# Linear attention and two MLPs on one core: the first MLP's weights converted two chunks at a time, all their lo parts on VectorE, and k's maximum as a tree

## The chip, the cores and the metric

The kernel runs on one core of one Trainium2 chip. The metric is the device time of one execution in microseconds (us); lower is better. The engines are named as in the profile: PE is TensorE's matmul, PEld its weight load, DVE VectorE, ACT ScalarE, POOL GpSimd, SP SyncE, which here only issues transfers (SPq).

## The reference, cut to what matters

```python
q_s = softmax(q, axis=-1); k_s = softmax(k, axis=2)      # (4, 8, 576, 64); over head_dim, over positions
kv = einsum("bhsd,bhse->bhde", k_s, v)
x = einsum("bhsd,bhde->bhse", q_s, kv)  -> (2304, 512)
x = (h - tanh(h)) @ moe_w_out,    h = x @ moe_w_in       # first MLP, d_ff 2048
x = softplus(h) @ moe2_w_out,     h = x @ moe2_w_in      # second MLP, same sizes
```

The weights reach the kernel as float64. All is computed to float32 accuracy: each matmul operand is split into a hi part in the rounded format float32r and a lo part, the float32 remainder, and each product is three matmuls (lo*hi, hi*lo, hi*hi).

## The kernel before, in words

The 2304 tokens are cut into five blocks of 512, 256, 512, 512 and 512. The first MLP walks through the blocks, and in each through d_ff in 16 chunks of 128 (a step is one chunk of one block). A step has 12 matmuls for the hidden layer (`hidden`, L323), the gate h - tanh(h) with its hi and lo part (`gate`, L332 to L335: ACT, DVE, ACT, DVE), and 12 matmuls that add the chunk to the block's output in four PSUM accumulators (`mid_out`, L350 to L352). `hidden` runs two steps ahead of `mid_out`. After the first MLP comes the second, which uses a Strassen-like scheme for its first matmul and takes the rest of the time.

The first block is also where the first MLP's weights are made. `w_task(f)` loads chunk f of `w_in` and of `w_out` as 64-bit words into two buffers of the tag "raw" (six of them, 4 KB per partition each), and two steps later turns each into float32 with `convert`: ACT writes sign and exponent material into the low words y (L121), DVE merges it with the sign of the high words x (L122), clamps x (L123), ACT scales x (L124), DVE shifts and merges (L125). `parts` then splits the float32 words: ACT copies the hi part (L131), and lo = x - hi (L132) runs on POOL, except for `w_in` of every fourth chunk, which runs on DVE. All of these work on 128 x 512 elements. The raw buffer is free once lo is done, and the next load into it waits for that on SP's queue. All weights stay in SBUF: `weights_out` holds `w_out`, the pools "first", "mid" and "last" hold `w_in`. The last two, and the pool "x1", lie where the prologue's tiles were.

In the fifth block, `w2_out_task` loads and converts the second MLP's `w_out` in the same way into the places of the first's, with lo on POOL (L155). In blocks three and four, `w2_in_task` converts the second `w_in`, builds its seven forms and writes them to DRAM (L189).

Attention for the next block runs beside the MLP's steps: `kv_task` (two heads each, four per batch) takes the maximum of k over positions in two stages. The first is a `tensor_reduce` on DVE over the six rows j that a partition holds (L229, 96 x 768 to 96 x 128, reading with j innermost, i.e. strided); then a transpose, a reduction over partitions, exp and the matmuls with v. `x_task` does q's softmax and multiplies by kv. A prologue does both for the first block, in an order written out by hand (`order`, L553), in which w0 and w1 are the conversions of chunks 0 and 1. Its x_tasks run two operations each on POOL (L281, L289).

Each engine works through its own queue in a fixed order, which the framework's planner sets at build time by the order of the program and the readiness of operands in its own cost model. Semaphores hold an instruction until its operands are there, and everything behind it on that engine waits too. `at(block, step, make)` says at which step a task starts; `yield` ends a task's share of a step.

Of the kernel before, what the change touches and what calls it, by code (L numbers as in the profile page):

```python
# [9 lines left out]
F32 = mybir.dt.float32  # L10
F32R = mybir.dt.float32r
U32 = mybir.dt.uint32
U16 = mybir.dt.uint16
AF = mybir.ActivationFunctionType
ALU = mybir.AluOpType
AX = mybir.AxisListType.X
# [3 lines left out]
def linear_attention_two_mlps(  # L20
# [28 lines left out]
    nc = tc.nc  # L49
    B, H, S, D = q.shape  # L50
    NT, DM = out.shape
    DFF = w1_in.shape[1] // 2
    P = 128
# [5 lines left out]
    NC = DM // P  # L59
    NF = DFF // P  # L60
    NHP = H // 2
    KP, KJ = 96, 6
# [26 lines left out]
    def f32(ap):  # L89
        return ap.bitcast(F32)  # L90
# [6 lines left out]
    weights = {}  # L97
    wi, wo = {}, {}

    def raw_tile(name):  # L100
        return main.tile([P, NC, 2 * P], U32, tag="raw", name=name, bufs=6)

    def load_in(raw, w_in, f):
        nc.sync.dma_start(
            out=raw, in_=w_in[:, 2 * f * P : 2 * (f + 1) * P].rearrange("(c p) f -> p c f", p=P)
        )

    def load_out(raw, w_out, f):
        nc.sync.dma_start(out=raw.rearrange("p c f -> p (c f)"), in_=w_out[f * P : (f + 1) * P, :])

    def convert(raw):

        words = raw.rearrange("p c (f two) -> p c f two", two=2)
        y, x = words[:, :, :, 0], words[:, :, :, 1]
        top = raw.bitcast(U16).rearrange("p c (f four) -> p c f four", four=4)[:, :, :, 1]  # L120
        nc.scalar.activation(y, top, AF.Copy, scale=2.0**-13, bias=2.0**-14 - 0.5)  # L121
        nc.vector.scalar_tensor_tensor(y, x, 0x80000000, y, op0=ALU.bitwise_and, op1=ALU.bitwise_or)  # L122
        nc.vector.tensor_scalar(f32(x), f32(x), MOST, -MOST, op0=ALU.min, op1=ALU.max)  # L123
        nc.scalar.mul(f32(x), f32(x), 2.0**-111)  # L124
        nc.vector.scalar_tensor_tensor(x, x, 3, y, op0=ALU.logical_shift_left, op1=ALU.bitwise_or)  # L125
        return f32(x)

    def parts(pool, w, m, f, x, eng):
        hi = pool.tile([P, NC, P], F32R, tag=f"{w}h{f}", name=f"{w}h{m}_{f}")
        lo = pool.tile([P, NC, P], F32R, tag=f"{w}l{f}", name=f"{w}l{m}_{f}")  # L130
        nc.scalar.copy(hi, x)  # L131
        eng.tensor_tensor(lo, x, f32(hi), op=ALU.subtract)  # L132
        return hi, lo

    def whole(t):
        return t.rearrange("p c f -> p (c f)")

    def w_task(f):
        raws = [raw_tile(f"raw{w}0_{f}") for w in "io"]
        load_in(raws[0], w1_in, f)  # L140
        load_out(raws[1], w1_out, f)
        yield
        yield
        pool = weights["first" if f < 4 else "last" if f >= 12 else "mid"]
        wi[f] = parts(pool, "i", 0, f, convert(raws[0]), nc.vector if f % 4 == 0 else nc.gpsimd)
        wo[0, f] = tuple(map(whole, parts(weights_out, "o", 0, f, convert(raws[1]), nc.gpsimd)))

    def w2_out_task(f):
        raw = raw_tile(f"rawo1_{f}")
        load_out(raw, w2_out, f)  # L150
        yield
        yield
        x = convert(raw)
        yield
        wo[1, f] = tuple(map(whole, parts(weights_out, "o", 1, f, x, nc.gpsimd)))  # L155

    forms = [dram.tile([P, NFORM, 2, 2 * P], F32, tag=f"forms{p}", name=f"forms{p}") for p in range(NF // 2)]

    def w2_in_task(p):


        raws = [raw_tile(f"rawi1_{f}") for f in PAIRS[p]]
        for raw, f in zip(raws, PAIRS[p]):
            load_in(raw, w2_in, f)
        yield
        yield
        w0 = convert(raws[0])
        yield
        w1 = convert(raws[1])
        yield  # L170
        sums = f32(raw_tile(f"sums{p}").rearrange("p c f -> p (c f)")).rearrange("p (s c f) -> p s c f", s=4, c=2)
        s2, s3, s1, s4 = (sums[:, i] for i in range(4))
        a11, a12, a21, a22 = w0[:, :2], w0[:, 2:], w1[:, :2], w1[:, 2:]
        nc.vector.tensor_tensor(s1, a21, a22, op=ALU.add)
        nc.vector.tensor_tensor(s2, s1, a11, op=ALU.subtract)
        nc.vector.tensor_tensor(s3, a11, a21, op=ALU.subtract)
        nc.vector.tensor_tensor(s4, a12, s2, op=ALU.subtract)
        yield
        flat = sums.rearrange("p s c f -> p s (c f)")
        for n, of in enumerate((w0, flat[:, :2], flat[:, 2:], a22)):  # L180
            size = 1 if n == 3 else 2
            t = main.tile([P, size, 2, 2 * P], F32R, tag="raw", name=f"stage{p}_{n}", bufs=6)
            hi, lo = t[:, :, 0], t[:, :, 1]
            if n in (0, 3):
                hi, lo = (v.rearrange("p s (c f) -> p s c f", c=2) for v in (hi, lo))
                of = of.rearrange("p (s c) f -> p s c f", c=2)
            nc.scalar.copy(hi, of)
            nc.vector.tensor_tensor(lo, of, f32(hi), op=ALU.subtract)
            nc.sync.dma_start(out=forms[p][:, 2 * n : 2 * n + size], in_=f32(t))  # L189
            yield  # L190
# [11 lines left out]
    def kv_task(b, hp, pool, bufs):  # L202


        nm = f"{b}_{hp}"

        def load(t, src):
            for h in range(2):
                nc.sync.dma_start(
                    out=t[:, :, h * D : (h + 1) * D], in_=src[b, 2 * hp + h].rearrange("(p j) d -> p j d", j=KJ)  # L210
                )

        if pool is att:
            kt = ke = pool.tile([KP, KJ, 2, D], F32, tag="k", name=f"k{nm}", bufs=bufs)
            load(kt.rearrange("p j h d -> p j (h d)"), k)
        else:
            whole = pool.tile([KP, 2, KJ, D], F32, tag="k", name=f"k{nm}", bufs=bufs)
            nc.sync.dma_start(
                out=whole.rearrange("p h j d -> p h (j d)"),
                in_=k[b, 2 * hp : 2 * hp + 2].rearrange("h (p j) d -> p h (j d)", j=KJ),  # L220
            )
            kt = whole.rearrange("p h j d -> p j h d")
            ke = pool.tile([KP, KJ, 2, D], F32, tag="ke", name=f"ke{nm}", bufs=bufs)
        yield
        vt = pool.tile([KP, KJ, P + 2], F32, tag="v", name=f"v{nm}", bufs=bufs)
        nc.gpsimd.memset(vt[:, :, P:], 1.0)
        load(vt, v)
        m1 = pool.tile([KP, 2, D], F32, tag="m1", name=f"m1{nm}", bufs=bufs)
        nc.vector.tensor_reduce(m1, kt.rearrange("p j h d -> p h d j"), axis=AX, op=ALU.max)  # L229
        yield  # L230
        pm = psum_a(f"pm{nm}")
        nc.tensor.transpose(pm[:, :KP], m1.rearrange("p h d -> p (h d)"), ident[:KP, :KP])
        mx = pool.tile([P, 1], F32, tag="mx", name=f"mx{nm}", bufs=bufs)
        nc.vector.tensor_reduce(mx, pm[:, :KP], axis=AX, op=ALU.max)
        yield
        pb = psum_a(f"pb{nm}")
        nc.tensor.transpose(pb[:KP, :P], mx.to_broadcast([P, KP]), ident)
        most = pb[:KP, :P].rearrange("p (h d) -> p h d", h=2).unsqueeze(1).to_broadcast([KP, KJ, 2, D])
        nc.vector.tensor_tensor(ke, kt, most, op=ALU.subtract)
        nc.scalar.activation(ke, ke, AF.Exp)  # L240
        yield
        pk = psum_a(f"pk{nm}")
        for j in range(KJ):
            nc.tensor.matmul(pk[:, : P + 2], ke[:, j].rearrange("p h d -> p (h d)"), vt[:, j], start=j == 0, stop=j == KJ - 1)
        r = pool.tile([P, 1], F32, tag="r", name=f"r{nm}", bufs=bufs)
        nc.vector.tensor_scalar(r, pk[:, P : P + 1], 1e-9, None, op0=ALU.add)
        nc.vector.reciprocal(r, r)
        for h in range(2):
            d = slice(h * D, (h + 1) * D)
            nc.scalar.mul(kv[b % 2, hp][d, d], pk[d, d], r[d])  # L250
# [268 lines left out]
    def at(block, step, make):  # L519
        starts.setdefault(block * NF + step, []).append(make)  # L520

    PRE = 2
    KV_AT, X_AT = (0, 3, 6, 9), (1, 4, 8, 10)
    for f in range(NF):
        if f >= PRE:
            at(0, f - 6, lambda f=f: w_task(f))
        if f < NF - 2:
            at(NB - 1, f - 1, lambda f=f: w2_out_task(ORDER[f]))
    for p in range(NF // 2):
# [19 lines left out]
    wide += ["h0", "acc", "a", "acc", "h1", "acc", "a", "acc"] * 2 + ["h0", "acc", "a", "acc"]  # L549
    tasks = {f"k{hp}": kv_task(0, hp, pro, NHP) for hp in range(NHP)}  # L550
    tasks |= {f"x{hp}": x_task(0, hp, pro, NHP) for hp in range(NHP)}
    tasks |= {f"w{f}": w_task(f) for f in range(PRE)}
    order = """k0 k1 k2 k3 x0 x1 x2 x3 k0 k0 k1 k1 w0 k2 k3 k2 k3 x1 k0 x0 k1 k0 x0 w0 x2 k2 x2 x3 x1 x3 w1 k3 w1 k1 x0 k2 x1 k3 x2 x3 x0 w0 x2 x3 w1 x1"""  # L553
    for n, name in enumerate(order.split()):
        next(tasks[name], None)
        if n == 7:
# [135 lines left out]
```

## Time and profile before

| | |
|---|---|
| median of 3 runs | 892.52 us (892.36 to 894.33) |
| profiled execution's own time | 893.67 us |
| its span, first to last instruction | 891.9 us |
| PE busy (share of the span) | 841.6 us (94%) |
| DVE busy | 637.8 us (72%) |
| ACT busy | 489.3 us (55%) |
| POOL busy | 93.0 us (10%) |

Busy times are averages over parts with different limits, so the rows further on go stretch by stretch. A busy PE need not be PE at full pace: a matmul record lasts longer when the clock is low, and its end is modelled. The first hidden matmul starts at 34.17 us. In the stretches used here, the prologue is 0 to 34 us, the first block 34 to 150, the second (256 tokens) 150 to 217, the third 217 to 315, the fourth 315 to 407, and the fifth with the change to the second MLP 407 to 511. The blocks overlap by two steps of `mid_out`.

### The profile page before, as it was taken

The page shows a single profiled execution, that of the slowest core. Times are in us where ns is not written, and L with a number is a line of the kernel's source. Part 1 is how long each engine was busy: PE and PEld are TensorE (multiplying, and loading weights), DVE is VectorE, ACT ScalarE, POOL GpSimd, SP SyncE. Part 2 cuts the span into 40 slices and gives each one's busy share as a digit, 9 for nine tenths or more (in the row PEclk, how much of TensorE's full clock was granted, in tenths as well). Part 3 has the DMA queues.
Part 4 walks back from the last instruction along what each step waited for, and adds up shares of the span by engine and source line. Part 5 has one row for each costly group of instructions (what it writes and reads, how often), then busy time and mean ns, then how long its engine had stood idle before and what let it go on. Part 6 is the DMA issues. An engine that isn't in the chain of part 4 may idle for free.

```text
span 891.9 us, 11576 instructions
## 1 busy us (share of the span) xinstructions
PE 841.6 (94%) x4152; PEld 721.9 (81%) x4152; DVE 637.8 (72%) x990; ACT 489.3 (55%) x806; POOL 93.0 (10%) x88
## 2 busy tenths in 40 slices
PE   4788889999999999999998999999999999999997
PEld 3566768998888888888886888988899989898986
DVE  8899999899897444434697475667957669675664
ACT  4877776555665332223563565647556466655643
POOL 4243431000000000001242300000100000000000
PEclk9899999999999999999999999999999999999999
DMA  9565655876664210003427254343653444543421
GB/s 248 160 183 170 182 144 145 261 207 186 245 227 134 51 47 12 12 1 118 155 71 249 83 175 112 114 129 113 198 174 111 125 113 124 183 124 111 115 59 71
DMA packets 98616, 121.34 MB, mean 136 GB/s; under 512 B 38656, under 2 KB 62976, under 8 KB 98560
## 3 DMA queue, kind: packets, MB, share of 16 engines
q1 hardware_dynamic: 98560, 120.61, 44.9%
q8 instruction: 33, 0.54, 0.3%
q14 instruction: 23, 0.19, 0.1%
HBM read 96.47 MB, written 24.12 MB: 135 GB/s over the span
## 4 chain that ended last, share of the span: by engine, by line
PE 63%; DVE 15%; issue 8%; DMA 5%; ACT 5%; POOL 3%; SPq 0%; POOLq 0%; ACTq 0%; DVEq 0%
PE h L323 11%; PE one L418 10%; PE o L495 7%; PE o L496 7%; PE o L494 7%; PE seven L418 5%; PE x L352 4%; PE x L350 4%; PE x L351 4%; PE two L418 2%; POOL ol L132 2%; DVE m L229 2%; DVE g L333 1%; DMA rawi<-in_moe_w_in_dram 1%; DVE rawi L122 1%
## 5 line engine op out<-in xcount | busy, mean ns | idle before, releaser
L323 PE MATMUL h<-xh,il 128*128 128x512 f32 (+1 forms) x320 | 126.9, 397 | 9.7 <-DVE g L333 4.4
L323 PE MATMUL h<-xl,ih 128*128 128x512 f32 (+1 forms) x320 | 120.7, 377 | 0.8 <-DVE xl L308 0.8
L323 PE MATMUL h<-xh,ih 128*128 128x512 f32 (+1 forms) x320 | 120.6, 377 | 0.0
L350 PE MATMUL x<-gh,ol 128*128 128x512 f32 (+1 forms) x320 | 119.2, 372 | 0.9 <-DVE x2s L359 0.9
L352 PE MATMUL x<-gh,oh 128*128 128x512 f32 (+1 forms) x320 | 118.7, 371 | 0.0
L351 PE MATMUL x<-gl,oh 128*128 128x512 f32 (+1 forms) x320 | 118.7, 371 | 0.0
L418 PE MATMUL one<-xf,wf 128*128 128x384 f32 x576 | 116.8, 337 | 0.9 <-ACT u L433 0.9
L494 PE MATMUL o<-oh,gl 128*128 128x512 f32 x288 | 112.8, 392 | 2.3 <-DVE gl L479 1.8
L495 PE MATMUL o<-ol,gh 128*128 128x512 f32 x288 | 113.7, 395 | 0.0
L496 PE MATMUL o<-oh,gh 128*128 128x512 f32 x288 | 113.7, 395 | 0.0
L418 PEld LDWEIGHTS one<-xf,wf 128*128 128x128 f32 x576 | 103.0, 188 | 7.4 <-ACT u L433 1.4
L333 DVE TENSOR_TENSOR g<-h,g 128x512 f32<-128x512 f32 (+1 forms) x80 | 50.6, 632 | 53.1 <-ACT g L332 52.9
L332 ACT ACTIVATE g<-h 128x512 f32<-128x512 f32 (+1 forms) x80 | 44.0, 549 | 76.9 <-PE h L323 76.7
L470 DVE TENSOR_SCALAR u<-e 128x768 f32<-128x768 f32 x48 | 26.7, 557 | 80.0 <-ACT e L468 80.0
L323 PEld LDWEIGHTS h<-xh,il 128*128 128x128 f32 x320 | 62.0, 194 | 23.7 <-DVE g L333 5.9
L323 PEld LDWEIGHTS h<-xl,ih 128*128 128x128 f32 x320 | 62.0, 194 | 11.8 <-DVE xl L308 1.6
L478 ACT CAST gh<-e 128x768 fp32r<-128x768 f32 x48 | 40.2, 837 | 56.8 <-DVE e L475 56.2
L323 PEld LDWEIGHTS h<-xh,ih 128*128 128x128 f32 x320 | 61.6, 192 | 10.9
L350 PEld LDWEIGHTS x<-gh,ol 128*128 128x128 f32 x320 | 61.0, 191 | 11.5 <-DVE x2s L359 1.5
L352 PEld LDWEIGHTS x<-gh,oh 128*128 128x128 f32 x320 | 60.9, 190 | 10.2
L351 PEld LDWEIGHTS x<-gl,oh 128*128 128x128 f32 x320 | 60.8, 190 | 10.0
L335 DVE TENSOR_TENSOR gl<-g,gh 128x512 fp32r<-128x512 f32 (+1 forms) x80 | 53.3, 666 | 20.1 <-ACT gh L334 18.9
(97 smaller groups left out, 1534.5 us busy)
## 6 DMA issues: line engine op xcount, KB each, us to landing
wf<-forms SPq DMA_DIRECT2D x168, 256.0 KB, 2.7
rawi<-in_moe_w_in_dram SPq DMA_DIRECT2D x32, 512.0 KB, 4.3
rawo<-in_moe_w_out_dram SPq DMA_DIRECT2D x32, 512.0 KB, 3.4
forms<-stage SPq DMA_DIRECT2D x24, 512.0 KB, 3.2
v<-in_v_dram SPq DMA_DIRECT2D x32, 144.0 KB, 3.9
out_dram<-ot SPq DMA_DIRECT2D x18, 256.0 KB, 3.0
x2d<-x2s SPq DMA_DIRECT2D x16, 256.0 KB, 2.2
k<-in_k_dram SPq DMA_DIRECT2D x24, 144.0 KB, 3.5
```

The source lines that it names most:

```text
L323: nc.tensor.matmul(p, w[:, c], x[:, c, :n], start=at == 0, stop=at == 3 * NC - 1)
L332: tanh[0] = nc.scalar.activation(g, h, AF.Tanh)
L333: nc.vector.tensor_tensor(g, h, g, op=ALU.subtract)
L335: nc.vector.tensor_tensor(gl, g, f32(gh), op=ALU.subtract)
L350: nc.tensor.matmul(a, ol[:, s], gh, start=first, stop=False)
L351: nc.tensor.matmul(a, oh[:, s], gl, start=False, stop=False)
L352: nc.tensor.matmul(a, oh[:, s], gh, start=False, stop=last)
L418: nc.tensor.matmul(a, w[:, wp, c], x[:, xp, c], start=first and at == 0, stop=at == 5, skip_group_check=True)
L478: nc.scalar.copy(gh, e)
L494: nc.tensor.matmul(a, gl[:, c], oh, start=first, stop=False)
L495: nc.tensor.matmul(a, gh[:, c], ol, start=False, stop=False)
L496: nc.tensor.matmul(a, gh[:, c], oh, start=False, stop=last)
```

## The change

- `w_task` now takes a pair of chunks (2p, 2p+1). It starts two steps earlier before its first chunk (f - 8 instead of f - 6, and four `yield`s instead of two), so that the conversion of a pair's first chunk comes at the same step as before. For `w_in` of pairs 2 to 6 and `w_out` of pairs 1 to 6 both chunks lie side by side, and each of the five conversion instructions, the hi copy and the lo subtraction run once on 128 x 1024 elements. For the others (`w_in` of pairs 0, 1 and 7, `w_out` of pairs 0 and 7) they run on 128 x 512 as before.
- The words of most pairs are loaded into the place that the hi and lo parts of a later pair will take (`IN_AT`, `OUT_AT`: pair 2's `w_in` words wait in pair 6's place, and so on). Only `w_in` of pairs 0, 1 and 7 and `w_out` of pair 7 use raw buffers.
- lo = x - hi always runs on DVE, in `w2_out_task` too.
- A pair's hi and lo parts are one tile, also in the second `w_out`: its first chunk's parts are written when both chunks of the first MLP in that place are no longer used.
- k's maximum over the six rows is a tree: three rows with three (384 elements), then two instructions on 128.
- In the prologue the four loads of chunks 0 and 1 are all issued at the first `w`, and `w` takes the places of w0 and w1's later shares in part.

```diff
+    def parts(out, x):
+        nc.scalar.copy(out[0], x)
+        nc.vector.tensor_tensor(out[1], x, f32(out[0]), op=ALU.subtract)
+    IN_AT, OUT_AT = {2: 6, 3: 7, 4: 5, 5: 6, 6: 7}, {0: 4, 1: 5, 2: 6, 3: 7, 4: 5, 5: 6, 6: 7}
-    def w_task(f):
...
-        wi[f] = parts(pool, "i", 0, f, convert(raws[0]), nc.vector if f % 4 == 0 else nc.gpsimd)
-        wo[0, f] = tuple(map(whole, parts(weights_out, "o", 0, f, convert(raws[1]), nc.gpsimd)))
+    def w_task(p):
+        f = 2 * p
+        raws = []
+        for w, at_, pool_of in (("i", IN_AT, in_pool), ("o", OUT_AT, lambda _: weights_out)):
+            if p in at_:
+                tag = at_[p]
+                raw = pool_of(tag).tile([P, 2, 2 * DM], U32, tag=f"{w}{tag}", name=f"raw{w}0_{f}")
+                raws.append([raw[:, k] for k in range(2)] if p == 0 else [raw.rearrange("p k f -> p (k f)")])
...
+        for k in range(2):
+            for n, (t, raw) in enumerate(zip(made, raws)):
+                if len(raw) == 2:
+                    parts([part[:, k] for part in (t[:, 0], t[:, 1])], f32(convert(raw[k])[1]))
+                elif k == n:
+                    parts([part.rearrange("p k f -> p (k f)") for part in (t[:, 0], t[:, 1])], f32(convert(raw[0])[1]))
+            yield
     def w2_out_task(f):
...
-        wo[1, f] = tuple(map(whole, parts(weights_out, "o", 1, f, x, nc.gpsimd)))
+        if f % 2 == 0:
+            out2[f] = out2[f + 1] = weights_out.tile([P, 2, 2, DM], F32R, tag=f"o{f // 2}", name=f"o1_{f}")
+        wo[1, f] = tuple(out2[f][:, n, f % 2] for n in range(2))
+        parts(wo[1, f], f32(x))
...
-        nc.vector.tensor_reduce(m1, kt.rearrange("p j h d -> p h d j"), axis=AX, op=ALU.max)
+        m3 = att.tile([KP, KJ // 2, 2, D], F32, tag="m3", name=f"m3{nm}") if pool is att else ke[:, : KJ // 2]
+        nc.vector.tensor_tensor(m3, kt[:, : KJ // 2], kt[:, KJ // 2 :], op=ALU.max)
+        nc.vector.tensor_tensor(m1, m3[:, 0], m3[:, 1], op=ALU.max)
+        nc.vector.tensor_tensor(m1, m1, m3[:, 2], op=ALU.max)
...
-        if f >= PRE:
-            at(0, f - 6, lambda f=f: w_task(f))
+        if f >= PRE and f % 2 == 0:
+            at(0, f - 8, lambda f=f: w_task(f // 2))
```

## Rows read from the trace of the kernel before

**Rows 1.** Busy time by stretch: stretch, length, each engine's busy us (instructions), clock, DMA.

```profile
34.00:150.00 116.00, 100.32 (x441) 80.52 (x441) 112.76 (x186) 81.83 (x147) 41.68 (x31) 0.94 0.56 160
150.00:217.00 67.00, 62.50 (x477) 58.81 (x476) 61.45 (x134) 40.30 (x88) 0.43 (x4) 1.00 0.68 211
217.00:315.00 98.00, 97.31 (x472) 80.15 (x471) 76.27 (x144) 51.47 (x93) 0.32 (x3) 1.00 0.51 166
...
460.00:511.00 51.00, 46.61 (x203) 38.08 (x202) 33.55 (x43) 26.15 (x45) 16.74 (x10) 0.97 0.43 146
```

**Rows 2.** Chain that ended last, fourth block: start us, us, what.

```profile
325.97 2.72 PE h L323 x12
...
331.41 2.72 PE h L323 x12
```

**Rows 3.** Instructions of DVE in time, first block: start us, us, what.

```profile
40.80 1.57 DVE L123 TENSOR_SCALAR rawi<-rawi 128x512 f32<-128x512 f32 x1
42.29 0.68 DVE L125 SCALAR_TENSOR_TENSOR rawo<-rawo 128x512 uint32<-128x512 uint32 x1
42.90 0.68 DVE L335 TENSOR_TENSOR gl<-g,gh 128x512 fp32r<-128x512 f32 x1
```

**Rows 4.** Instructions of POOL in time, first block.

```profile
40.77 1.32 POOL L132 TENSOR_TENSOR il<-rawi,ih 128x512 fp32r<-128x512 f32 x1 [3.39 <-ACT ih L131]
```

**Rows 5.** Line L123 alone: count, ns min/median/max, first and last start us.

```profile
L123 DVE TENSOR_SCALAR rawi<-rawi x32: 403/422/1578, 22.2 to 253.4; 128x512 f32<-128x512 f32 x32
```

**Rows 6.** Groups of DVE by shape, 25 to 150 us: count, busy us, mean ns, idle before.

```profile
L122 DVE SCALAR_TENSOR_TENSOR rawi<-rawi 128x512 uint32<-128x512 uint32 x19 | 17.8, 938 | 0.8 <-ACT rawi L121 0.8
L125 DVE SCALAR_TENSOR_TENSOR rawi<-rawi 128x512 uint32<-128x512 uint32 x18 | 15.9, 881 | 0.4 <-ACT rawi L124 0.3
L123 DVE TENSOR_SCALAR rawi<-rawi 128x512 f32<-128x512 f32 x18 | 13.1, 727 | 0.0
L125 DVE SCALAR_TENSOR_TENSOR rawo<-rawo 128x512 uint32<-128x512 uint32 x16 | 12.6, 788 | 0.0
L335 DVE TENSOR_TENSOR gl<-g,gh 128x512 fp32r<-128x512 f32 x15 | 12.5, 834 | 0.9 <-ACT gh L334 0.8
L122 DVE SCALAR_TENSOR_TENSOR rawo<-rawo 128x512 uint32<-128x512 uint32 x15 | 11.3, 754 | 0.0
L333 DVE TENSOR_TENSOR g<-h,g 128x512 f32<-128x512 f32 x16 | 10.9, 680 | 1.3 <-ACT g L332 1.3
...
L289 DVE TENSOR_TENSOR qn<-q,qsum 128x256 f32<-128x256 f32 x4 | 3.8, 960 | 0.0
...
L281 DVE TENSOR_TENSOR q<-q,qm 128x256 f32<-128x256 f32 x4 | 3.0, 746 | 0.0
```

**Rows 7.** Groups of POOL by shape, 25 to 150 us.

```profile
L132 POOL TENSOR_TENSOR ol<-rawo,oh 128x512 fp32r<-128x512 f32 x16 | 25.0, 1564 | 32.1 <-ACT oh L131 32.1
L132 POOL TENSOR_TENSOR il<-rawi,ih 128x512 fp32r<-128x512 f32 x12 | 18.8, 1568 | 33.6 <-ACT ih L131 28.9 <-DMA q<-in_q_dram 4.7
```

**Rows 8.** DVE in time: two of 256 elements, then two of 768, back to back.

```profile
143.54 0.42 DVE L176 TENSOR_TENSOR sums<-rawi,rawi 128x256 f32<-128x256 f32 x1
143.88 0.42 DVE L177 TENSOR_TENSOR sums<-rawi,sums 128x256 f32<-128x256 f32 x1
...
459.44 0.94 DVE L384 TENSOR_TENSOR xf<-t,xf 128x768 fp32r<-128x768 f32 x1
460.31 0.94 DVE L384 TENSOR_TENSOR xf<-xs,xf 128x768 fp32r<-128x768 f32 x1
```

**Rows 9.** DVE in time: the prologue's four reductions of k.

```profile
4.25 5.51 DVE L229 TENSOR_REDUCE m<-k 96x128 f32<-96x768 f32 x4 [4.25 <-DMA k<-in_k_dram]
```

**Rows 10.** Prologue in time: SP's issue of the later v; PE's first hidden matmuls.

```profile
11.99 3.38 SPq L209 DMA_DIRECT2D v<-in_v_dram  x4
...
34.17 1.22 PE L323 MATMUL h<-xh,il 128*128 128x512 f32 x2 [4.20 <-POOL il L132]
```

**Rows 11.** Waits, 405 to 512 us: who for whom, us in total, times, longest.

```profile
PE h L323 <- DVE g L333: 4.4, 2, 2.9
...
ACT oh L131 <- PE x L352: 2.4, 3, 0.9
```

**Rows 12.** Groups of POOL, 405 to 512 us.

```profile
L132 POOL TENSOR_TENSOR ol<-rawo,oh 128x512 fp32r<-128x512 f32 x15 | 23.0, 1535 | 58.3 <-ACT oh L131 53.1 <-DVE gl L335 5.2
```

More of the change, by code (lines that the diff above doesn't have):

```diff
@@ L108, in load_out @@
     def load_out(raw, w_out, f):
-        nc.sync.dma_start(out=raw.rearrange("p c f -> p (c f)"), in_=w_out[f * P : (f + 1) * P, :])
+        nc.sync.dma_start(out=raw, in_=w_out[f * P : (f + 1) * P, :])
     def convert(raw):
-        words = raw.rearrange("p c (f two) -> p c f two", two=2)
-        y, x = words[:, :, :, 0], words[:, :, :, 1]
-        top = raw.bitcast(U16).rearrange("p c (f four) -> p c f four", four=4)[:, :, :, 1]
+        words = raw.rearrange("p (f two) -> p f two", two=2)
+        y, x = words[:, :, 0], words[:, :, 1]
+        top = raw.bitcast(U16).rearrange("p (f four) -> p f four", four=4)[:, :, 1]
         nc.scalar.activation(y, top, AF.Copy, scale=2.0**-13, bias=2.0**-14 - 0.5)
@@ L125, in convert @@
         nc.vector.scalar_tensor_tensor(x, x, 3, y, op0=ALU.logical_shift_left, op1=ALU.bitwise_or)
[L126 to L136, printed above, removed]
@@ L138, in w_task, with in_pool @@
-    def w_task(f):
-        raws = [raw_tile(f"raw{w}0_{f}") for w in "io"]
-        load_in(raws[0], w1_in, f)
-        load_out(raws[1], w1_out, f)
+        return y, x
+    def parts(out, x):
+        nc.scalar.copy(out[0], x)
+        nc.vector.tensor_tensor(out[1], x, f32(out[0]), op=ALU.subtract)
+    def in_pool(p):
+        return weights["first" if p < 2 else "last" if p >= 6 else "mid"]
+    IN_AT, OUT_AT = {2: 6, 3: 7, 4: 5, 5: 6, 6: 7}, {0: 4, 1: 5, 2: 6, 3: 7, 4: 5, 5: 6, 6: 7}
[7 more added lines that the diff above has]
+                raws.append([raw[:, k] for k in range(2)] if p == 0 else [raw.rearrange("p k f -> p (k f)")])
+                each = [raw[:, k] for k in range(2)]
+            else:
+                each = [raw_tile(f"raw{w}0_{f + k}").rearrange("p c f -> p (c f)") for k in range(2)]
+                raws.append(each)
+            for k in range(2):
+                if w == "i":
+                    load_in(each[k].rearrange("p (c f) -> p c f", c=NC), w1_in, f + k)
+                else:
+                    load_out(each[k], w1_out, f + k)
@@ L142, in w_task @@
         yield
         yield
-        pool = weights["first" if f < 4 else "last" if f >= 12 else "mid"]
-        wi[f] = parts(pool, "i", 0, f, convert(raws[0]), nc.vector if f % 4 == 0 else nc.gpsimd)
-        wo[0, f] = tuple(map(whole, parts(weights_out, "o", 0, f, convert(raws[1]), nc.gpsimd)))
+        if p:
+            yield
+            yield
+        made = []
+        for w, pool in (("i", in_pool(p)), ("o", weights_out)):
+            made.append(pool.tile([P, 2, 2, DM], F32R, tag=f"{w}{p}", name=f"{w}0_{f}"))
@@ new lines, in w_task @@
+        for k in range(2):
+            wi[f + k] = tuple(made[0][:, n, k].rearrange("p (c f) -> p c f", c=NC) for n in range(2))
+            wo[0, f + k] = tuple(made[1][:, n, k] for n in range(2))
+        for k in range(2):
+            for n, (t, raw) in enumerate(zip(made, raws)):
[3 more added lines that the diff above has]
+                    parts([part.rearrange("p k f -> p (k f)") for part in (t[:, 0], t[:, 1])], f32(convert(raw[0])[1]))
+            yield
@@ L148, in w2_out_task @@
     def w2_out_task(f):
-        raw = raw_tile(f"rawo1_{f}")
+        raw = raw_tile(f"rawo1_{f}").rearrange("p c f -> p (c f)")
         load_out(raw, w2_out, f)
@@ L152, in w2_out_task @@
         yield
-        x = convert(raw)
+        _, x = convert(raw)
         yield
-        wo[1, f] = tuple(map(whole, parts(weights_out, "o", 1, f, x, nc.gpsimd)))
+        if f % 2 == 0:
+            out2[f] = out2[f + 1] = weights_out.tile([P, 2, 2, DM], F32R, tag=f"o{f // 2}", name=f"o1_{f}")
+        wo[1, f] = tuple(out2[f][:, n, f % 2] for n in range(2))
+        parts(wo[1, f], f32(x))
+    out2 = {}
     forms = [dram.tile([P, NFORM, 2, 2 * P], F32, tag=f"forms{p}", name=f"forms{p}") for p in range(NF // 2)]
@@ L166, in w2_in_task @@
         yield
-        w0 = convert(raws[0])
+        w0, w1 = (raw.rearrange("p c (f two) -> p c f two", two=2)[:, :, :, 1] for raw in raws)
+        w0, w1 = f32(w0), f32(w1)
+        convert(raws[0].rearrange("p c f -> p (c f)"))
         yield
-        w1 = convert(raws[1])
+        convert(raws[1].rearrange("p c f -> p (c f)"))
         yield
@@ L551, in linear_attention_two_mlps @@
     tasks |= {f"x{hp}": x_task(0, hp, pro, NHP) for hp in range(NHP)}
-    tasks |= {f"w{f}": w_task(f) for f in range(PRE)}
-    order = """k0 k1 k2 k3 x0 x1 x2 x3 k0 k0 k1 k1 w0 k2 k3 k2 k3 x1 k0 x0 k1 k0 x0 w0 x2 k2 x2 x3 x1 x3 w1 k3 w1 k1 x0 k2 x1 k3 x2 x3 x0 w0 x2 x3 w1 x1"""
+    tasks["w"] = w_task(0)
+    order = """k0 k1 k2 k3 x0 x1 x2 x3 k0 k0 k1 k1 w k2 k3 k2 k3 x1 k0 x0 k1 k0 x0 w x2 k2 x2 x3 x1 x3 k3 k1 x0 k2 x1 k3 x2 x3 x0 w x2 x3 w x1"""
     for n, name in enumerate(order.split()):
```

## The prediction

> **What bounds the kernel now.** I read the busy time by stretch first. In the fourth block PE is the bound: its chain steps from one group of 12 hidden matmuls to the next in 331.41 - 325.97 = 5.44 us [rows 2], so 16 steps take 87.0 us. The third block has the same steps plus attention, and PE is busy for 97.31 of its 98 us; attention therefore adds about 98 - 87 = 11 us of PE time to a block [rows 1]. The first block does the same work in 116 us, 18 us more than 98. There DVE is busy for 112.76 of 116 us, ACT for 81.83 [rows 1]: the first block runs at the pace of DVE's queue, and what DVE is spared or given there is what the block is worth. The second block, half as wide, is mixed: DVE busy for 61.45 of 67 us, PE for 62.50 [rows 1].
>
> Next I looked at what DVE does in the first block. Two neighbours of 512 elements start 0.61 us apart when nothing disturbs them, but the clamp at 40.80 us holds the engine for 1.49 us [rows 3], and POOL's lo subtraction runs from 40.77 to 42.09 us [rows 4]. The clamp's own statistics are bimodal, median 422 ns and longest 1578 [rows 5]. A DVE instruction that meets a POOL subtraction is held until this ends. The gate's subtraction L333, which reads PSUM, keeps 680 ns on average in the same stretch, while L335, which reads two SBUF operands, goes to 834 [rows 6]. So POOL's share is paid for by DVE.
>
> **The change part by part.** All terms are us of DVE time in the first block unless another place is named.
>
> *Stalls that go.* POOL has 16 + 12 = 28 subtractions between 25 and 150 us [rows 7]. What they cost DVE is the mean of each group over its undisturbed length, times its count [rows 6]. Undisturbed are 680 ns (512 elements; L333 in the same rows, and rows 3), 422 ns for L123 [rows 5] and 420 ns for 256 elements [rows 8]. L122: 258 ns x 19 + 74 x 15 = 6.0. L125: 201 x 18 + 108 x 16 = 5.3. L123: 305 x 18 = 5.5. L335: 154 x 15 = 2.3. L289: 540 x 4 = 2.2. L281: 326 x 4 = 1.3. Sum 22.6 us, 0.81 us for each POOL subtraction. With POOL idle all of it goes; at the other end, if something else made these instructions long, none goes. I take 22.6, because the long ones lie beside POOL's work and L333 does not have them.
>
> *Subtractions that come.* From 256 and 768 elements, 0.34 and 0.87 us start to start [rows 8], DVE's spacing is about 0.073 us + 1.04 ns per element: 0.605 for 512, 1.137 for 1024. Afterwards there are 11 double ones (5 of w_in, 6 of w_out) and 10 single ones (6 and 4), 11 x 1.137 + 10 x 0.605 = 18.5, less the four that DVE does already (2.4): +16.1. One lo part costs DVE 0.57 to 0.6 us when it does it itself and 0.81 us when POOL does it.
>
> *Merging.* The other three DVE instructions of a conversion are merged in the same 11 pairs: 33 x 0.073 = -2.4. ACT saves as many fixed shares, but it has room. The price is granularity: a gate's subtraction can now stand behind one of 1.14 us, which the two steps that `hidden` runs ahead cover (10.9 us). By the Trainium skill (VectorE: DVE Perf Modes, The TRN2 errata) a VectorE instruction pays 151 cycles beside its elements, 0.157 us. By that a merge would be worth 0.157 instead of 0.073, and the sum some 3.7 us better (an estimate); the record lengths here fit it (0.68 us for 512), but the spacing of starts does not, and spacing is what a full queue pays.
>
> *k's maximum.* Four reductions take 5.51 us, 1.38 each [rows 9]. The tree has 384 + 128 + 128 elements: 0.47 + 0.20 + 0.20 = 0.87, a saving of 0.51. If each of the dependent three waited out its record (0.08 longer than its spacing [rows 8]) it would be 0.27. I take 0.51, since two neighbours of 256 in which one needs an earlier result keep 0.34 [rows 8]. Four in the first block: -2.0. Four in the second, where DVE is busy for 92%: -1.8. Four in the third, where PE is the bound: 0. Four in the prologue: between 0 and -2.0, as the tiles of k land one after the other and the last sets the end; I take -1.0. By the Trainium skill (VectorE: DVE Perf Modes, Rules for kernel authors, and the cost formula under The TRN2 errata) a reduction runs at one element per cycle, (768 + 151) / 0.96 = 0.96 us, and the tree's three instructions would take 1.14: the tree would then be a loss of 0.18 each, and the total below would come to about -10 instead of -16.7 (an estimate). The row says 1.38, so the strided read here is slower than the page's rate, and the row decides.
>
> *Loads.* Words that wait in later places are asked for two steps earlier and without a wait for raw buffers. As DVE is 97% busy in the first block [rows 1], late words are not what bounds it, and I cost this at 0; should DVE fall idle, the deeper prefetch is what keeps words at hand. In the prologue two more loads of 512 KB stand on SP's queue ahead of the last four loads of v, now issued from 11.99 us [rows 10]. That is 1 MB more; at the first block's 160 GB/s [rows 1] it takes 6.6 us, but these loads of v serve the last two head pairs only, and the first hidden matmul at 34.17 us has waited 4.20 us for chunk 1's lo part on POOL [rows 10], which now comes sooner. Between -3 and +3; I take 0.
>
> *Fifth block.* The second w_out has 15 lo parts on POOL in 405 to 512 us [rows 12], moved to DVE at 0.605 each, 9.1 us. DVE is busy for only 33.55 of 51 us between 460 and 511 [rows 1], so it has room, and POOL's holds on it go. PE idles for 51.00 - 46.61 = 4.4 us there [rows 1], and waits for the gate's DVE part for 4.4 us in two pieces [rows 11]. Between 0 and -4.4; I take -3, as two POOL subtractions of x2_task stay.
>
> **Sum.** First block: -22.6 + 16.1 - 2.4 - 2.0 = -10.9. Prologue -1.0, second block -1.8, fifth -3.0. Together -16.7. The profiled execution took 893.67 us (span 891.9); 877.0 by that, and as the median of the runs lies 1.15 us lower, **876 us**. The block would then take 105 us, above PE's 98, with DVE near 97% and ACT near 78%. So DVE still bounds it, by less, and what is late next is the gate behind conversions.
>
> **The rivals.**
>
> *PE becomes the bound.* DVE's holds hit instructions that the planned order did not expect to be long; without them PE may follow its plan as it does in the third block. First block 98 instead of 116: -18. Second block 43.5 + 11 = 54.5 instead of 67: -12.5. Prologue -2, fifth -4.4. Together -36.9, about 855 us. For it: in the third block DVE is 78% busy and costs PE next to nothing. Against it: the sum leaves DVE 7 us above PE in the first block.
>
> *The gain is spent on other work.* The raw buffers are nearly unused by the first MLP, so `w2_in_task` can load early, and the planner may put its DVE work into the first block. One pair is two conversions and the forms: 2 x (0.605 + 0.34 + 0.605) + 4 x 0.34 + 3 x 0.605 + 0.34 = 6.6 us. One and a half pairs eat the first block's gain, and only what the second block is spared comes back: 883 to 890. Against it: this work must be done anyway, and DVE is less loaded later.
>
> *Slower: the pair's place in the fifth block.* A hi copy of the second w_out may be written only when both chunks of the pair are done, so every even chunk's copy is free one step (5.44 us) later than now. It sits in ACT's queue with the gate's tanh and hi copy behind it. ACT already waits there for PE, three times, 2.4 us in all [rows 11]. If each of the 8 copies comes half a step early, 8 x 2.72 = 21.8 us, against 13.7 us gained before: about 901. It decides from 1.7 us per copy on. Against it: the planner knows when the place is free and can put the tanh first.
>
> *The change doesn't do what it says.* The holds have another cause and stay: 16.1 - 2.4 - 2.0 - 1.0 - 1.8 = +8.9, 901 us. The pairing of rows 3 and 4 speaks against it.
>
> **How the numbers follow.** DVE's sum 0.56, PE bound 0.20, gain spent 0.15, the pair's place 0.06, holds that stay 0.03. What this kernel's measurement can tell from no change is 0.3%, 2.7 us: faster is below 889.8, slower above 895.2. Faster gets 0.56 + 0.20 + 0.10 = 0.86, the same 0.05 from the third case, slower 0.09. For DVE's sum alone I expect 868 to 883; the range of 8 in 10 takes in the upper half of the PE case and the spent gain: 858 to 888.
>
> **What would show it.** Right, step by step: L122, L123, L125 and L335 at 0.68, 0.42, 0.68 and 0.68 us in every instance of 512 elements; no L132 on POOL; double instructions spaced near 1.14 us; k's three instructions at 0.87 us together; the first block at 105 us, DVE above 95% busy in it; PE idle less than 2 us between 460 and 511. Wrong: long DVE instructions with POOL idle; a first block of 98 us or 116 us; ACT waiting for PE before the hi copies of the second w_out; a first hidden matmul later than 35 us.

## The result, and the profile after

The changed kernel takes 867.26 us (median of 4 runs) against 892.52; the ratio is 0.9698, 95% interval [0.9662, 0.9733]. The forecast was 876 us, within 858 to 888. One far longer run among the four (924.48 us) was disturbed and is left out of the ratio. The profiled execution has a span of 865.8 us against 891.9.

The busy time of the changed kernel by block, cut where the first hidden matmul of each block starts (columns as in [rows 1]: PE, PEld, DVE, ACT, POOL, clock, DMA share, GB/s):

```profile
32.90:130.50 97.60, 94.75 (x438) 75.28 (x437) 93.94 (x158) 73.07 (x107) 0.42 (x4) 0.99 0.55 170
130.50:191.90 61.40, 61.16 (x477) 58.45 (x476) 58.21 (x143) 40.93 (x88) 0.42 (x4) 1.00 0.69 215
191.90:295.30 103.40, 99.04 (x476) 81.45 (x474) 81.49 (x169) 56.23 (x101) 0.32 (x3) 0.98 0.59 186
295.30:387.50 92.20, 92.20 (x411) 75.06 (x410) 33.14 (x54) 26.55 (x44) 0.00 (x0) 1.00 0.05 18
387.50:485.90 98.40, 98.40 (x441) 82.12 (x440) 67.45 (x102) 53.40 (x88) 7.18 (x3) 1.00 0.43 150
```

The same cuts in the kernel before lie at 34.2, 149.9, 216.4, 314.8 and 407.0 us, and its fifth block with the first MLP's last matmul ends at 512.3. So the time went like this:

| part | before | after | difference | forecast |
|---|---|---|---|---|
| prologue | 34.2 | 32.9 | -1.3 | -1.0 |
| first block | 115.8 | 97.6 | -18.2 | -10.9 |
| second | 66.4 | 61.4 | -5.0 | -1.8 |
| third | 98.4 | 103.3 | +4.9 | 0 |
| fourth | 92.2 | 92.2 | 0 | 0 |
| fifth, to its last matmul | 105.2 | 98.4 | -6.8 | -3.0 |
| rest (second MLP) | 379.6 | 379.9 | +0.3 | 0 |

In the first block PE's clock is back at 0.99 (0.94 before [rows 1]), DVE is still busy for 93.94 of 97.60 us and POOL does nothing but small memsets. DVE's conversion instructions in the changed kernel from 25 to 150 us, which answer to [rows 6] (columns as there):

```profile
L376 DVE TENSOR_TENSOR gl<-g,gh 128x512 fp32r<-128x512 f32 x16 | 10.8, 679 | 0.0
L127 DVE SCALAR_TENSOR_TENSOR rawo<-rawo 128x1024 uint32<-128x1024 uint32 x6 | 7.3, 1222 | 0.2 <-ACT rawo L126 0.2
L133 DVE TENSOR_TENSOR o<-rawo,o 128x1024 fp32r<-128x1024 f32 x6 | 7.3, 1219 | 0.0
L124 DVE SCALAR_TENSOR_TENSOR rawo<-rawo 128x1024 uint32<-128x1024 uint32 x6 | 7.3, 1216 | 0.0
...
L124 DVE SCALAR_TENSOR_TENSOR rawi<-rawi 128x512 uint32<-128x512 uint32 x8 | 5.4, 680 | 0.0
...
L125 DVE TENSOR_SCALAR rawi<-rawi 128x512 f32<-128x512 f32 x8 | 3.3, 413 | 0.1
```

Every group has its undisturbed length: 680 ns for 512 elements, 1.22 us for 1024, 413 ns for the clamp (L125; 727 before). The gate's L376 has gone from 834 to 679 ns without an edit of its own.

The third block's loss has a place. PE in the changed kernel, start us, us, what:

```profile
231.17 0.40 PE L364 MATMUL h<-xh,i 128*128 128x512 f32 x1
234.55 0.27 PE L273 MATMUL pm<-ident,m 96*128 96x96 f32 x1 [2.98 <-DVE m L270]
234.61 0.47 PE L364 MATMUL h<-xh,i 128*128 128x512 f32 x1
```

A transpose of k's maximum stands in PE's queue between hidden matmuls and waits 2.98 us for DVE. The chain of releases that leads to it begins with words of the second w_in (start us, us, what):

```profile
223.77 6.22 DMA rawi<-in_moe_w_in_dram
...
230.01 0.67 ACT rawi L123
230.71 0.69 DVE rawi L124
...
232.60 0.46 DVE m L268
...
234.21 0.21 DVE m L270
```

ACT and DVE wait for these words. The two loads of k, issued at 224.25 and 224.88 us, had landed by 231.3 us; only at 232.52 us does DVE's queue reach the first instruction of its tree, and the other two stand behind further conversions and a gate's subtraction. Two windows of that trace, the first just behind, show what follows:

```profile
235.90:238.90 3.00, 3.00 (x8) 2.31 (x7) 1.54 (x3) 1.01 (x2) 0.00 (x0) 0.50 0.00 0
240.00:243.00 3.00, 3.00 (x15) 2.42 (x14) 2.60 (x7) 0.96 (x3) 0.00 (x0) 1.00 0.43 175
```

After the wait the granted clock is 0.50 (1.2 GHz), and 8 matmuls stand in 3 us instead of 15.

### The profile page after: what moved, and what is told of

Same layout as the page of the kernel before. It is cut to its first block, busy times and chain, and to the rows that moved or that the text cites. A ratio compares the mean times of both kernels' runs of the same rounds, so it can differ in the third digit from the quotient of the medians.

```text
span 865.8 us, 11436 instructions
## 1 busy us (share of the span) xinstructions
PE 835.5 (97%) x4152; PEld 717.6 (83%) x4152; DVE 620.0 (72%) x1022; ACT 485.3 (56%) x773; POOL 25.1 (3%) x44
## 4 chain that ended last, share of the span: by engine, by line
PE 76%; DVE 9%; ACT 7%; DMA 6%; issue 1%; SPq 0%; ACTq 0%; DVEq 0%
PE h L364 17%; PE one L459 10%; PE o L536 7%; PE o L537 7%; PE o L535 7%; PE x L391 6%; PE x L393 6%; PE x L392 6%; PE seven L459 5%; PE two L459 3%; DMA rawi<-in_moe_w_in_dram 2%; PE px L346 2%; PE pk L285 1%; DMA forms<-stage 1%; DMA k<-in_k_dram 1%
## 5 line engine op out<-in xcount | busy, mean ns | idle before, releaser
L364 PE MATMUL h<-xh,i 128*128 128x512 f32 (+1 forms) x640 | 202.9, 380 | 1.2 <-DVE i L133 0.7
L364 PEld LDWEIGHTS h<-xh,i 128*128 128x128 f32 x640 | 117.9, 189 | 24.6 <-DVE i L133 2.4
L364 PE MATMUL h<-xl,i 128*128 128x512 f32 (+1 forms) x320 | 119.1, 372 | 0.0
L392 PE MATMUL x<-gl,o 128*128 128x512 f32 (+1 forms) x320 | 118.8, 371 | 0.0
L393 PE MATMUL x<-gh,o 128*128 128x512 f32 (+1 forms) x320 | 118.6, 371 | 0.0
L391 PE MATMUL x<-gh,o 128*128 128x512 f32 (+1 forms) x320 | 115.8, 370 | 0.5 <-ACT gh L375 0.5
L535 PE MATMUL o<-o,gl 128*128 128x512 f32 x288 | 112.6, 391 | 2.8 <-DVE gl L520 2.3
L536 PE MATMUL o<-o,gh 128*128 128x512 f32 x288 | 113.6, 395 | 0.0
L537 PE MATMUL o<-o,gh 128*128 128x512 f32 x288 | 113.6, 395 | 0.0
L364 PEld LDWEIGHTS h<-xl,i 128*128 128x128 f32 x320 | 60.8, 190 | 10.8 <-issue 1.5
L391 PEld LDWEIGHTS x<-gh,o 128*128 128x128 f32 x320 | 60.4, 189 | 10.8 <-ACT gh L375 0.9
L392 PEld LDWEIGHTS x<-gl,o 128*128 128x128 f32 x320 | 60.6, 189 | 10.3 <-DVE gl L376 0.4
L393 PEld LDWEIGHTS x<-gh,o 128*128 128x128 f32 x320 | 60.4, 189 | 9.7
L535 PEld LDWEIGHTS o<-o,gl 128*128 128x128 f32 x288 | 54.0, 188 | 10.9 <-DVE gl L520 3.2
```

Source lines behind the costliest of these rows:

```text
L364: nc.tensor.matmul(p, w[:, c], x[:, c, :n], start=at == 0, stop=at == 3 * NC - 1)
L391: nc.tensor.matmul(a, ol[:, s], gh, start=first, stop=False)
L392: nc.tensor.matmul(a, oh[:, s], gl, start=False, stop=False)
L393: nc.tensor.matmul(a, oh[:, s], gh, start=False, stop=last)
L535: nc.tensor.matmul(a, gl[:, c], oh, start=first, stop=False)
L536: nc.tensor.matmul(a, gh[:, c], ol, start=False, stop=False)
```

## The experiments

The theory: a lo part on POOL costs DVE a hold of 0.8 us, more than making it on DVE, and that is where most of the time came from. Its rivals: the loads into later places with the merging; the tree; a better planned queue. All ratios are against the kernel before, on one chip in each group of four kernels.

| kernel | median us | ratio [95%] | first / second / third / fifth block, us |
|---|---|---|---|
| lo parts alone | 872.63 | 0.9749 [0.9715, 0.9783] | 104.7 / 63.3 / 99.1 / 98.4 |
| changed, lo parts back | 885.76 | 0.9893 [0.9851, 0.9936] | 119.9 / 62.3 / 97.0 / 103.1 |
| changed, no merging | 872.94 | 0.9757 [0.9715, 0.9800] | 104.1 / 61.8 / 101.3 / 98.4 |
| changed, no tree | 868.76 | 0.9711 [0.9676, 0.9746] | 102.1 / 62.9 / 98.7 / 98.4 |
| changed, POOL echoes | 884.44 | 0.9874 [0.9837, 0.9911] | 119.3 / 61.4 / 101.4 / 98.4 |
| changed, POOL writes only | 866.79 | 0.9678 [0.9644, 0.9712] | 101.6 / 61.4 / 100.0 / 98.4 |
| changed, second w_out's lo back | 869.94 | 0.9712 [0.9673, 0.9751] | 98.9 / 61.4 / 102.5 / 102.3 |
| changed, k's maximum a step later | 867.17 | 0.9685 [0.9642, 0.9728] | 99.1 / 62.7 / 99.2 / 98.4 |
| changed, again | 865.65 | 0.9688 [0.9659, 0.9717] | 98.1 / 61.4 / 100.3 / 98.4 |
| later step for the last batch only | 862.72 | 0.9641 [0.9617, 0.9666] | 97.2 / 61.4 / 97.9 / 98.4 |
| form loads held back | 861.63 | 0.9642 [0.9615, 0.9669] | 97.7 / 65.1 / 97.0 / 98.4 |
| both of the last two | 864.39 | 0.9660 [0.9636, 0.9683] | 98.0 / 62.9 / 97.8 / 98.4 |

**The lo parts alone**, in the kernel before:

```diff
-        wi[f] = parts(pool, "i", 0, f, convert(raws[0]), nc.vector if f % 4 == 0 else nc.gpsimd)
+        wi[f] = parts(pool, "i", 0, f, convert(raws[0]), nc.vector)
-        ... parts(weights_out, "o", 0, f, convert(raws[1]), nc.gpsimd)     # and the second w_out
+        ... parts(weights_out, "o", 0, f, convert(raws[1]), nc.vector)
```

> The kernel before with one edit: every lo part of the weights (first MLP and second w_out) on VectorE; loads, raw buffers, single-chunk conversions and k's reduction as before. Theory holds (a lo part costs DVE 0.81 us as a hold when POOL makes it, 0.6 us when DVE does): first block about 5 to 14 us shorter (22.6 of holds against 16.9 of added work, more if the second MLP's form work leaves the block), fifth about 5, time 874 to 882. Rival places (the gain came from loads into later places and from merging): no gain, DVE's queue longer, 890 to 900.

Just below the theory's window: this edit alone gives 2.5% of the 3.0%, about 23 us. All of the fifth block's gain is there, and 11 of the first block's 18 us.

**The lo parts back on POOL**, in the changed kernel (in pieces of 512 elements):

```diff
-        nc.vector.tensor_tensor(out[1], x, f32(out[0]), op=ALU.subtract)
+        for k, eng in enumerate(engs):      # POOL, but DVE for w_in of every fourth chunk
+            eng.tensor_tensor(lo[k], of[k], f32(hi[k]), op=ALU.subtract)
```

> The changed kernel with one edit back: lo parts on POOL for the same 28 chunks of the first MLP and for the second w_out, in pieces of 512 elements; merged conversions, later places and the tree stay. Theory holds: the long L124, L125, L127 instructions are back, first block 108 to 116 us instead of 97.6, time 882 to 890. Rival places: 866 to 872, as without the edit.

The time is the theory's. The first block grows to 119.9 us, more than expected, and the holds are back. Two groups of DVE from 25 to 150 us in this kernel; the clamp on 1024 elements takes 688 ns in the changed one:

```profile
L381 DVE TENSOR_TENSOR gl<-g,gh 128x512 fp32r<-128x512 f32 x16 | 14.3, 896 | 0.0
...
L125 DVE TENSOR_SCALAR rawi<-rawi 128x1024 f32<-128x1024 f32 x5 | 6.8, 1354 | 0.0
```

With the lo parts on POOL, merging, places and tree together bring 1.1%.

**POOL echoes.** POOL repeats the 28 subtractions of chunks into dead words. DVE's queue is, instruction by instruction, that of the changed kernel, so a better plan cannot be what differs:

```diff
+        again, of, hi = y, x, out[0]        # the low words y are not read any more
+        nc.gpsimd.tensor_tensor(again, of, f32(hi), op=ALU.subtract)
```

> The changed kernel, and POOL repeats the subtraction for the 28 chunk parts it had before, writing into the dead low words, which nobody reads; DVE's queue is that of the changed kernel. Theory holds: DVE is held 0.8 us by each, 22 us in all, the first block has 97.6 us with DVE full, so it goes to 114 to 120, time 884 to 890. Rival plan (the holds cost little, the gain of the changed kernel came from a better planned queue): 867 to 871.

The theory's case. The first block is 119.3 us instead of 97.6, with DVE full; its busy time there is 117.31 us (93.94 in the changed kernel):

```profile
32.10:151.40 119.30, 103.76 (x438) 79.48 (x437) 117.31 (x159) 74.73 (x110) 56.82 (x31) 0.93 0.44 139
```

The pairing is plain in time. DVE, then POOL, of this kernel:

```profile
46.08 0.69 DVE L133 TENSOR_TENSOR i<-rawi,i 128x512 fp32r<-128x512 f32 x1
46.69 2.35 DVE L124 SCALAR_TENSOR_TENSOR rawi<-rawi 128x1024 uint32<-128x1024 uint32 x1
48.97 2.33 DVE L133 TENSOR_TENSOR o<-rawo,o 128x1024 fp32r<-128x1024 f32 x1
...
46.12 1.83 POOL L151 TENSOR_TENSOR rawi<-rawi,i 128x512 f32<-128x512 f32 x1 [5.73 <-ACT i L132]
47.91 4.55 POOL L151 TENSOR_TENSOR rawo<-rawo,o 128x512 f32<-128x512 f32 x2
```

Two DVE instructions of 1.22 us take 2.35 and 2.33 us while POOL subtracts. Taken one by one, DVE's instructions up to 200 us are 23.5 us longer in sum than the same ones of the changed kernel, and each that is more than 0.15 us longer overlaps an instruction of POOL. SP's next loads wait for POOL too (8.5 us in all between 20 and 152 us), but DVE idles for only 2 us in the block, so late words are not what it costs. POOL's work feeds nobody; it costs about 18 us only by being there.

**POOL writes only**: the same places, two memsets each instead of the subtraction.

```diff
-        nc.gpsimd.tensor_tensor(again, of, f32(hi), op=ALU.subtract)
+        for j in range(2):
+            nc.gpsimd.memset(again.bitcast(U32), 0)
```

> As the echo, but POOL only writes: two memsets of the dead low words for each of the 28 chunk parts, some 1.1 us together. If reading on POOL is what holds DVE: no long DVE instructions, 866 to 870. If any POOL access to SBUF holds it: 0.4 to 0.8 us for each, 875 to 888.

Neither as stated. DVE instructions with two inputs keep their length, but the clamp does not (groups of this kernel, 25 to 150 us):

```profile
L125 DVE TENSOR_SCALAR rawi<-rawi 128x1024 f32<-128x1024 f32 x5 | 7.8, 1564 | 0.0
...
L133 DVE TENSOR_TENSOR o<-rawo,o 128x1024 fp32r<-128x1024 f32 x6 | 7.3, 1210 | 0.0
```

So a write on POOL holds the clamp and not the two-input instructions. Four of these five clamps meet memsets. One of them, DVE then POOL:

```profile
59.30 2.13 DVE L125 TENSOR_SCALAR rawi<-rawi 128x1024 f32<-128x1024 f32 x1
58.84 2.04 POOL L152 MEMSET rawo<- 128x512 uint32 x4 [3.89 <-DVE rawo L127]
```

The first block takes 101.6 us with DVE busy for 97.93, 4 us more than in the changed kernel; the medians do not tell the two kernels apart.

**No merging**: conversions work on 512 elements, in the later places all the same.

```diff
-  raws.append([raw[:, k] for k in range(2)] if p == 0 else [raw.rearrange("p k f -> p (k f)")])
+  raws.append([raw[:, k] for k in range(2)])
```

> The changed kernel, but every conversion, hi copy and lo part works on one chunk (512 elements); loads still go to the later places. Theory holds: DVE gets 44 x 0.073 = 3.2 us more, the first block has PE as its bound and little room on DVE, so 0 to 4 us slower, 866 to 871. Rival merging is the source: 875 or more.

More than the theory said. The first block is 104.1 us, and DVE works 99.04 us in it, 5.1 more than in the changed kernel; 3.2 of it are the fixed shares, and about 1.2 are two more conversion instructions of the second w_in that start there. The block's loss is clear: four executions with the changed kernel's DVE queue in this block and an idle POOL (the changed kernel twice, the second w_out's lo back, the later step for the last batch only) took 97.2 to 98.9 us. For the whole time it is not shown: the interval overlaps that of the changed kernel, only just in its second round, [0.9659, 0.9717]. By the medians merging would be worth 5 to 7 us.

**No tree**: the strided reduction again.

> The changed kernel with k's maximum as the strided reduction again. Theory: 0.5 us of DVE back for each of the 8 in blocks one and two and 1 us in the prologue, part of it covered by PE, 867 to 872. Rival tree is the source: 877 or more. By the Trainium skill's cost formula the tree would be a loss, and this kernel 1 to 3 us faster than the changed one.

Not told apart from the changed kernel (0.9711 against 0.9698, intervals overlapping). The first block is 102.1 us, outside the 97.2 to 98.9 above, and the second 62.9, but the third is 98.7: there PE waits 1.4 us for k's maximum, against 4.4 in the changed kernel.

**The second w_out's lo parts back on POOL.**

> The changed kernel with only the second w_out's 16 lo parts back on POOL. Theory: first four blocks as in the changed kernel, the fifth with its tail 103 to 105 us instead of 98.4, time 871 to 874. Rival (the fifth block's gain came from the first MLP's earlier end): 867.

The fifth block goes from 98.4 to 102.3 us, so in this kernel 3.9 of its 6.8 us are the lo parts there. In the kernel before, the lo parts alone brought all 6.8; why the two differ is open. The median is just below the window and the interval overlaps the changed kernel's.

**k's maximum a step later**, in the tasks beside the blocks:

```diff
         load(vt, v)
+        if pool is att:        # for the last batch only: if b == 3
+            yield
```

> The changed kernel with one more step between k's load and k's maximum in the tasks beside the blocks, so that PE's transpose is planned behind the landing. Theory of the third block (PE waits 4.4 us at two transposes for k that has just landed, then runs at the lower clock for a while): third block 98 to 99 us instead of 103.3, time 861 to 865. Rival: the wait moves to the matmuls with kv, 866 to 870.

The third block falls to 99.2 us, and the first, second and fourth give that back (99.1, 62.7 and 93.3): the rival's time, though the wait did not move to the matmuls with kv alone. For the last batch only:

> The changed kernel with the added step between k's load and its maximum for the last batch only (the tasks of the third block). Theory of the third block's wait: first two blocks as in the changed kernel (97.6 and 61.4 us), third 99 instead of 103.3, time 862 to 865. Rival: it moves, 866 to 868.

> The changed kernel once more, beside the next ones on one chip: 865 to 869.

The third block is 97.9 us and the first two stay, while the fourth is 93.3 instead of 92.2. PE's waits for k's maximum, 4.4 us in the changed kernel's third block, are gone from it. The time is 862.72 us against 865.65 on the same chip, but the intervals [0.9617, 0.9666] and [0.9659, 0.9717] overlap, and the third block of the changed kernel itself differs between executions, 103.3 and 100.3 us.

**Form loads held back**: the loads of the second w_in stand behind the last store of the second or third block's output.

```diff
+        with tc.issue_after(stored[1 + p // 4].ins):
             for raw, f in zip(raws, PAIRS[p]):
                 load_in(raw, w2_in, f)
```

> The changed kernel with the loads for the second MLP's forms held on SP's queue behind the last store of the second block's output (pairs 0 to 3) or of the third's (pairs 4 to 7), so that this DVE work (6.6 us a pair) leaves the second block and goes to the third and fourth, where DVE idled for 60 us. Theory: the second block was bound by DVE (58.5 of 61.4 us) because of it and falls to 55 to 57; third 97 to 100; fourth still 92 to 94; time 855 to 861. Rival: the second block has another bound, or the third takes the loss over, 865 to 868.

The theory on the second block fell. All form work is gone from it, and it is longer:

```profile
129.90:195.10 65.20, 63.06 (x478) 60.04 (x476) 40.29 (x96) 26.65 (x60) 0.42 (x4) 0.97 0.31 78
195.10:292.00 96.90, 96.90 (x474) 80.38 (x474) 70.48 (x145) 48.71 (x87) 0.32 (x3) 1.00 0.44 139
```

DVE is busy for 40 of 65 us there, PE for 63, so the form work did not set the block's length. PE is busy for 61.16 us in the changed kernel, and the block takes 61.4 us there and in five of the other kernels, so PE bounds it at about 61. Why it is longer here is seen only in part: PE waits once for 1.6 us for ACT's copy of the first block's output, and the granted clock is 0.97. The third block is back at 97 us without the waits for k's maximum. The ratio of 0.9642 is better than the changed kernel's 0.9688 by its median, but the intervals overlap.

> Both edits, the held loads and the added step for the last batch: theory 854 to 859, the third block at 97 to 98 us; rival 865 to 868.

Both together do not add up: 864.39 us. Versions at 0.964 to 0.966 exist, then, better than both kernels by their medians, but none is told apart from the changed kernel: the intervals overlap.

## Why the prediction was right, point by point

*What bounds.* DVE's queue set the first block's length, as read from [rows 1] and [rows 3]. In both kernels the block is DVE's work plus a few us: 112.76 of 116 us before, 93.94 of 97.60 after. Where a run puts work back on DVE the block grows with it: 97.74 of 102.1 us without the tree, 99.04 of 104.1 without merging, 117.31 of 119.3 with the echo.

*Stalls that go.* Right in cause and in size. The long instructions are gone. The echo shows the cause on an unchanged queue: 23.5 us of longer instructions against the 22.6 of the sum, and a first block of 97.6 us goes back to 119.3.

*Subtractions that come, merging.* The spacing of a double instruction is 1.14 us as worked out, and the lo parts cost what was said. The fixed shares (2.4 us for the conversions, 3.2 with the lo parts) were too little for merging by the run without it, whose first block is 6.5 us longer. What it brings beyond them and the two conversions named there is not settled.

*The first block as a whole* was mis-sized: -18.2 instead of -10.9. What failed is the silent step that the rest of DVE's work stays where it is. The second MLP's form work left the block. Instructions that write or read the tile "sums", and then "stage", in the first block of the kernel before (busy us and count on DVE, then ACT; one DVE instruction is in both rows), and "stage" in the changed kernel:

```profile
34.20:149.90 115.70, 2.21 (x5) 0.62 (x1) 0.94 0.56 160
34.20:149.90 115.70, 1.38 (x2) 1.28 (x2) 0.94 0.56 160
```

```profile
32.90:130.50 97.60, 0.00 (x0) 0.00 (x0) 0.99 0.55 170
```

With the conversions that feed them (three chunks' worth, 9 instructions, 4.7 us) some 7 us of this work lay in the first block before, and about 1 us after. Where the lo parts run decides it: with them alone moved to DVE there is no work on "sums" or "stage" in the first block, and with them back on POOL in the changed kernel it is there again ("sums", then "stage"):

```profile
29.50:149.40 119.90, 2.92 (x6) 1.23 (x2) 0.92 0.54 168
29.50:149.40 119.90, 2.46 (x4) 2.31 (x4) 0.92 0.54 168
```

My reading, not shown, is that the planner doesn't know of the holds: with the lo parts on POOL it saw DVE with room in the first block and filled it, and afterwards it sees DVE full. The rival that feared the opposite, "the gain is spent on other work", was wrong in sign. With this the block came to the 98 us of the rival "PE becomes the bound", with DVE at 96%: the two limits met. A first block of 98 us was among the prediction's own signs of being wrong, and it came; what it refutes is that DVE would still bound the block at 105 us, not the holds.

*k's maximum.* A tree takes 1.16 us when nothing lies between its dependent instructions (starts 4.20 and 5.36 us), and 0.47 + 0.20 + 0.20 us in a full queue. DVE, changed kernel:

```profile
4.20 0.56 DVE L268 TENSOR_TENSOR ke<-k 96x384 f32<-96x384 f32 x1 [4.20 <-DMA k<-in_k_dram]
4.79 0.29 DVE L269 TENSOR_TENSOR m<-ke 96x128 f32<-96x128 f32 x1
5.11 0.29 DVE L270 TENSOR_TENSOR m<-m,ke 96x128 f32<-96x128 f32 x1
5.36 0.56 DVE L268 TENSOR_TENSOR ke<-k 96x384 f32<-96x384 f32 x1
...
60.06 0.55 DVE L268 TENSOR_TENSOR m<-k 96x384 f32<-96x384 f32 x1
60.53 1.22 DVE L127 SCALAR_TENSOR_TENSOR rawi<-rawi 128x1024 uint32<-128x1024 uint32 x1
61.67 0.28 DVE L269 TENSOR_TENSOR m<-m 96x128 f32<-96x128 f32 x1
61.87 0.68 DVE L374 TENSOR_TENSOR g<-h,g 128x512 f32<-128x512 f32 x1
```

Both bounds were right, one for each place. By the Trainium skill (VectorE: DVE Perf Modes, the cost formula under The TRN2 errata) the tree would have been a loss, the prediction's estimate says. The kernel without it is not faster (868.76 us) and its first block is longer, which is against that; how much of the whole time the tree gains is below what the medians can tell.

*Second block.* -5.0 instead of -1.8. It is bound by PE near 61 us, as the held loads show; before, PE waited there for DVE for 4.4 us, 2.7 of them for k's maximum. The 54.5 us of the rival "PE becomes the bound", half a block and all of attention, was too low a floor. How much of that lateness came out of the first block was not tested.

*Third block.* Forecast 0, measured +4.9: a wait that the sum has no term for. PE's transpose stands ahead of what DVE has ready: DVE first waits for words of the second w_in and then reaches k's tree 1.2 us after k has landed, so it is not k's landing alone, as the runs' expectations put it. The lower clock follows. In the third block before, PE waited 0.7 us for k's maximum, afterwards 4.4. In another execution of the changed kernel the block took 100.3 us with 3.0 us of such waits, so part of it comes and goes.

*Fifth block.* -6.8 instead of at most -4.4: the bound took only PE's idle time, and PE's busy time fell as well, from 100.91 to 98.40 us. Part of that is the clock. In the kernel before the granted clock was 0.83 between 470 and 480 us, where PE waits for the gate; in the changed kernel it is 1.00 over the whole block. The block before, then these 10 us of it:

```profile
407.00:512.30 105.30, 100.91 (x442) 82.94 (x441) 68.61 (x88) 53.40 (x89) 29.97 (x18) 0.98 0.42 142
470.00:480.00 10.00, 7.09 (x25) 5.46 (x24) 6.33 (x8) 4.25 (x7) 2.61 (x2) 0.83 0.63 225
```

The lo parts there are 3.9 to 6.8 of the 6.8 us, by the two runs on them. The slower rival did not come: ACT waits for PE before the hi copies twice, 1.5 us in all, against three times and 2.4 us [rows 11].

```profile
ACT o L132 <- PE x L393: 1.5, 2, 0.8
```

*The total.* The profiled spans differ by 26.1 us, the sum said 16.7. The first, second and fifth blocks gave 14.3 us more than forecast and the third took 4.9 us back, so the number is nearer than its parts. The prologue's -1.3 tells nothing: in the second execution of the changed kernel it takes 31.0 us, 1.9 less than in the first.

## What to carry to other kernels

Before giving work to POOL to spare DVE, look for DVE instructions of one line with two lengths, and where the long ones lie beside POOL's, compare the sum of the holds with what the work would cost on DVE. Where a planner fills queues by its own cost model, a cost that it doesn't know can hurt twice: it holds the engine, and it may invite other work into the same stretch. A saving in a block counts until the next engine's floor; read that floor from a block of the same size (98 us from the third block before, 97.6 measured). The floor of the second block, reckoned from halves, missed (54.5 us, 61.4 measured).

## What the runs showed of the hardware that was not expected

POOL's memsets hold DVE's clamp (one tensor input, 688 ns undisturbed; 1564 on average over five, four of which meet memsets), and leave DVE's two-input instructions at 1.21 us; POOL's subtractions hold both. The Trainium skill (GPSIMD Engine Reference, Key points) says that POOL shares its SBUF interfaces with VectorE, with contention for 2-port and two-input DVE instructions. The runs agree, and add that it depends on what POOL does: its writes alone hold only the first kind.

A POOL subtraction of 512 elements took 1.30 us undisturbed but 3.88 us once at 463.90 us in the kernel before, when DVE ran two-input instructions back to back. The hold works both ways.

A DVE instruction that needs the result of the one just ahead started 0.59 us after it at 384 elements and 0.32 us at 128 (4.20 to 5.11 us in the changed kernel); with other work between, the next start came after 0.47 and 0.20 us. A planner that interleaves them gains 0.3 us a tree.
